# FFN weight scales from sums of squares of a second copy, and a reordered Strassen down phase with two-row-tile additions

## The chip, the core and the metric

The kernel is one program on one NeuronCore of a Trainium2 chip. The metric is the device time of one execution in microseconds (us), lower is better. The core has TensorE (PE, matrix products; its weight loads are shown as PEld), VectorE (DVE), ScalarE (ACT), GpSimd (POOL), and SyncE (SP), which here only issues DMAs. Every engine works through its own instructions in order and waits for the others by semaphores. The units' matmuls write PSUM, eight banks of 128 x 512 float32 numbers; DVE and ACT empty them.

## What is computed

One transformer block over 2048 tokens of width 576: pre-layernorm softmax attention with 32 heads of 18, and then a gated feed-forward network (FFN) of inner width 4608, each with a residual.

```python
h = x + _A_ref(_layernorm(x, axis=-1), A_wqkv, A_wo)
h2 = h + _B_ref(_layernorm(h, axis=-1), B_w_gate, B_w_up, B_w_down)

def _B_ref(x, w_gate, w_up, w_down):
    g = jnp.einsum("bsd,df->bsf", x, w_gate)
    u = jnp.einsum("bsd,df->bsf", x, w_up)
    h = _gelu(g) * u
    return jnp.einsum("bsf,fd->bsd", h, w_down)
```

The change lies in the FFN, and in the preparation of its scales beside the start of the attention.

## The kernel before

**Numbers.** Each float32 operand is multiplied by a power of two and cut into a float16 high part and a float16 rest, so that a product takes three float16 matmuls. The power of two of a weight block is found from its largest magnitude by `exponents`: DVE reduces (L129), a PE transpose of the column of maxima (L138), a second DVE reduce (L142), and some ten tiny integer operations.

**The loop.** The inner width is cut into 18 chunks of 256 columns; two chunks make one pass of the loop `for sc in range(9)`. The tokens are in two halves, p = 0 and p = 1. A full pass runs these stages in this order: `unit(c, 1)`, `unit(c + 1, 1)`, `down7(1)`, `unit(c + 2, 0)`, `unit(c + 3, 0)`, `down7(0)`, where c = 2 sc and the last three stages belong to the next pair of chunks. The first pass has the plain `down(1)` in place of `down7(1)`; the last one ends at `down7(1)`.

**A unit** multiplies half of the tokens by one chunk of the gate and the up matrix with seven Strassen products each: 14 products of 7 matmuls, alternating between gate (g) and up (u). They are numbered 0 to 13 below. Products 0, 4, 8 and 10 share PSUM bank g[0], products 1, 5, 9 and 11 share u[0]. Between them ACT copies the bank out: after product 0 to `xg` (L1198), after 1 to `xu` (L1201), after 4 to `ag` (L1213), after 5 to `au` (L1217), after 8 to `bg` (L1226), after 9 to `bu` (L1230). So product 10 waits until ACT has done the copy `bg`, and product 11 for the copy `bu`. ACT also applies gelu (L1180) and rounds seven results to their high parts (`high`, L1191); DVE adds, multiplies gate by up (L1183) and subtracts (last of all L1266 and L1267); POOL forms the seven rests (`low`, L1194). Six of the seven rests come behind product 11.

**A weight matrix** is loaded into the one buffer `W8` by `load_matrix` (eight DMAs on SP, L977 and L979; blocks A12, A22, A11, A21 in this order). POOL adds the four Strassen sums S1 to S4 (L993); the last one, S4, still reads A12. ACT rounds in three cuts (L1013: first the four loaded blocks' A12, A22, A11, then S1 and S2, then S3 and S4), DVE makes the rests (L1027, L1029). After the first cut's rests the load of the next matrix is issued into the same buffer. The rows of `w_down` use the same space (`load_down`, L1076); `split_down7` scales them (ACT L1136), forms sums (POOL L1138 to L1145), and cuts seven blocks (ACT L1132, DVE L1133).

**down7** multiplies by seven blocks of `w_down` for two row tiles at a time, 12 matmuls of 288 columns for a block, into three pairs of PSUM banks: X, B and Z. After each product DVE adds the bank to the running sum `nat` (L1291, or L1296 for two halves at once). Tiles of `nat` leave for DRAM (L1301), and the other half's come back (L1320).

**What sets the order.** PE, ACT, DVE, POOL and, in the FFN, SP run in the order in which the program text emits. `beside(main, side)` emits one step of the side work after each product of the unit. So the place where a side step is emitted is its place in the queue of every engine it uses. In the kernel before, the sums of the next gate matrix are formed beside `unit(c, 1)`, its cuts beside `unit(c + 1, 1)`, the rest of the splits is spread over `down7(1)` and the units of half 0, and `split_down7` stands in `unit(c + 3, 0)`.

## Time and profile before

| | us |
|---|---|
| median of 3 runs | 2756.2 |
| lowest and highest run | 2752.95, 2759.34 |
| the profiled execution's own time | 2758.85 |
| its span on the core | 2757.0 |

The profile is a record of one execution. A row of its timeline gives the start in us, the duration, the engine, the source line, the operation with its output and inputs, the number of instructions merged into the row, and in brackets the idle time before it and what ended that. A row of its table by stretches of time gives, for each stretch, its length, the busy time of PE, PEld, DVE, ACT and POOL with the number of instructions, the mean granted clock of PE, the share of the DMA engines, and GB/s. A row of its groups gives busy time and mean ns of one, and behind the bar the idle time of the engine before these instructions.

### The profile page before, as it was taken

Reading aid. Unit: us, or ns where it says so; the run is one execution under the profiler, and the core shown is the slowest. Engines: PE = TensorE matmul, PEld = TensorE weight load, DVE = VectorE, ACT = ScalarE, POOL = GpSimd, SP = SyncE. Lnnn points to the kernel's source line nnn. Section 1 sums busy time; section 2 is a strip of 40 time slices with the busy share of each in tenths; the row PEclk is TensorE's granted clock in tenths of the full one; section 3 lists DMA queues with packets and bytes.
Section 4 is the critical chain, followed back from the end, with each engine's and each line's share of the span. In section 5 each row is a group of like instructions: output and inputs, shape, how many; then the busy total and the mean of one; then the engine's idle time right before and its main releaser. Section 6 shows DMA issues by size and latency. Waiting matters only on the chain.

```text
span 2757.0 us, 54241 instructions
## 1 busy us (share of the span) xinstructions
PE 2594.8 (94%) x20381; PEld 1174.7 (43%) x20381; DVE 2321.2 (84%) x4230; ACT 1740.0 (63%) x3260; POOL 1034.9 (38%) x1274
## 2 busy tenths in 40 slices
PE   8999999999999999999999988898989898988989
PEld 4533333333333333333355545454445454544545
DVE  7479999999999999998676778788787878787885
ACT  6229999999999999997744334343343433343432
POOL 4202532323232323235853344444443334434432
PEclk9999999999999999999999999999999999999999
DMA  8521010101010101011344223222222223232212
GB/s 221 139 90 30 19 44 16 44 16 42 16 45 16 44 17 42 18 30 36 70 99 88 73 80 101 97 70 76 91 90 90 99 88 107 80 111 86 79 62 82
DMA packets 204761, 189.06 MB, mean 69 GB/s; under 512 B 92504, under 2 KB 151404, under 8 KB 204498
## 3 DMA queue, kind: packets, MB, share of 16 engines
q1 hardware_dynamic: 195758, 169.27, 20.6%
q0 software_dynamic: 8608, 16.33, 2.4%
q8 instruction: 159, 2.61, 0.4%
q14 instruction: 104, 0.85, 0.1%
q10 hardware_dynamic: 132, 0.01, 0.0%
HBM read 115.44 MB, written 50.40 MB: 60 GB/s over the span
## 4 chain that ended last, share of the span: by engine, by line
PE 70%; DVE 16%; issue 5%; ACT 3%; DMA 2%; POOL 2%; SPq 1%; DVEq 0%; ACTq 0%; POOLq 0%
PE bank L673 18%; PE more L1175 8%; PE bank L1175 7%; PE quad L615 7%; PE bank L615 6%; PE more L1286 4%; PE bank L1286 4%; PE quad L300 4%; PE quad L665 4%; PE bank L300 4%; PE bank L665 3%; DVE mx L625 3%; PE more L300 1%; DMA A<-in_B_w_up_dram 1%; DVE W L1029 1%
## 5 line engine op out<-in xcount | busy, mean ns | idle before, releaser
L667 ACT ACTIVATE WK<-quad 128x512 f32<-128x512 f32 x1170 | 656.3, 621 | 26.0 <-PE quad L665 23.6
L673 PE MATMUL bank<-WK,V 128*32 128x256 f32 x8192 | 607.7, 389 | 2.6 <-DVE nat L688 0.6
L625 DVE TENSOR_REDUCE mx<-quad 128x1 f32<-128x512 f32 x836 | 554.0, 685 | 9.0 <-PE quad L665 1.5
L667 ACT ACTIVATE WK<-bank 128x512 f32<-128x512 f32 x878 | 504.9, 622 | 12.0 <-PE bank L665 10.2
L625 DVE TENSOR_REDUCE mx<-bank 128x1 f32<-128x512 f32 x716 | 477.3, 685 | 35.5 <-PE bank L615 26.8
L1175 PEld LDWEIGHTS <-W 128*128 128x128 f16 x2394 | 242.6, 101 | 341.4 <-issue 85.5
L673 PEld LDWEIGHTS bank<-WK,V 128*32 128x32 f32 x8192 | 190.4, 109 | 268.5 <-issue 201.9
L698 POOL TENSOR_TENSOR rp<-rc,minus_one 128x4 f32<-128x4 f32 x112 | 111.2, 1012 | 380.1 <-DMA rc<-nat 377.9
L1175 PE MATMUL bank<-X,W 128*128 128x512 f16 x792 | 225.3, 382 | 0.0
L993 POOL TENSOR_TENSOR A<-A 128x384 f32<-128x384 f32 x136 | 142.7, 1065 | 193.3 <-DVE V L1208 99.3
L1175 PE MATMUL bank<-V,W 128*128 128x512 f16 x720 | 212.3, 395 | 0.5 <-ACT WK L1217 0.5
L615 PE MATMUL quad<-W 54*128 54x512 f16 x514 | 191.3, 383 | 0.0
L1286 PEld LDWEIGHTS <-WK 128*128 128x128 f16 x1472 | 147.3, 100 | 97.1 <-issue 54.2
L1286 PE MATMUL more<-nat,WK 128*128 128x288 f16 x736 | 142.4, 294 | 48.6 <-DVE nat L1291 48.6
L615 PEld LDWEIGHTS <-W 54*128 54x128 f16 x1024 | 74.5, 94 | 241.8 <-issue 227.5
L1013 ACT ACTIVATE W<-A,p_s_m 128x768 f16<-128x768 f32 (+1 forms) x78 | 79.0, 1036 | 149.1 <-DVE p_s_m L173 149.1
L665 PE MATMUL quad<-A 56*128 56x512 f16 x584 | 172.4, 381 | 0.3
L615 PE MATMUL quad<-A 54*128 54x512 f16 x462 | 171.8, 383 | 0.1
L615 PEld LDWEIGHTS <-A 54*128 54x128 f16 x1024 | 71.2, 94 | 231.5 <-issue 216.5
L665 PE MATMUL quad<-W 56*128 56x512 f16 x586 | 168.2, 382 | 0.1
L1175 PE MATMUL more<-V,W 128*128 128x512 f16 x414 | 125.3, 439 | 36.0 <-ACT nat L1226 16.9
L615 PE MATMUL bank<-A 54*128 54x512 f16 x442 | 152.3, 383 | 1.9 <-DMA A<-qk_hi 1.8
(460 smaller groups left out, 5136.7 us busy)
## 6 DMA issues: line engine op xcount, KB each, us to landing
nat_d<-nat SPq DMA_DIRECT2D x120, 288.0 KB
nat<-nat_d SPq DMA_DIRECT2D x120, 288.0 KB
A<-in_B_w_down_dram SPq DMA_DIRECT2D x8, 1152.0 KB
nat<-rc SPq DMA_DIRECT2D x32, 256.0 KB
A<-in_B_w_gate_dram SPq DMA_DIRECT2D x64, 128.0 KB
A<-in_B_w_up_dram SPq DMA_DIRECT2D x64, 128.0 KB
qk_hi<-tmp SPq DMA_DIRECT2D x36, 128.0 KB
qk_lo<-tmp SPq DMA_DIRECT2D x36, 128.0 KB
```

The source lines that it names most:

```text
L300: nc.tensor.matmul(dst, a, b, start=(i == 0), stop=(i == len(pairs) - 1))
L615: nc.tensor.matmul(pm[:, :TB], Q[r, q0 : q0 + P], keys, start=True, stop=True)
L625: nc.vector.tensor_reduce(dst, pm[:, :TB], axis=AX.X, op=ALU.max)
L665: nc.tensor.matmul(pS[:, :TB], K[r, kt * P : (kt + 1) * P], Q[r, qc * TB : (qc + 1) * TB], start=True, stop=True)
L667: nc.scalar.activation(pes[(2 * kt + hh // 2) % NPE][:, hh % 2], pS[:, :TB], AF.Exp, scale=ex_reg)
L673: nc.tensor.matmul(acc[32 * hh : 32 * hh + 32, qs], Vg[n // NB][:, kt * G4 + hh * VC : kt * G4 + hh * VC + 32], pes[(2 * kt + hh // 2) % N ...
L698: nc.gpsimd.tensor_tensor(rc[:, c : c + 4], den[:, c : c + 4], minus_one.to_broadcast([P, 4]), op=ALU.pow)
L993: op(W8[:, d], W8[:, a], W8[:, b])
L1013: by = hi_on or (lambda dst, src, k: nc.scalar.activation(dst, src, AF.Copy, scale=k))
L1029: nc.vector.scalar_tensor_tensor(wh[r, a:b, 2], W8[r, a:b, 2], s[r], wh[r, a:b, 2], op0=ALU.mult, op1=ALU.subtract)
L1175: nc.tensor.matmul(bank, w, x_, start=start and i == 0, stop=i == len(mm) - 1, skip_group_check=not start)
L1286: nc.tensor.matmul(bank[:, :HALF], a, b, start=start and k == 0, stop=k == len(mm) - 1, skip_group_check=not start)
```

## The change

Five things are changed.

1. The power of two of a gate, up or down block in chunks 2 and above comes from the sum of its squares instead of its largest magnitude. A second copy of the weights is loaded for it, squared in place by ACT with a sum along the row, and summed over the partitions by one matmul with ones. `scan_weights` does it for two gate and two up chunks beside `unit(c, 1)`, `scan_down` for the two down chunks beside `unit(c + 2, 0)`, both in the space of the `nat` tiles that are in DRAM at the time; those tiles are loaded behind it. `next_norms` does it for the chunks 2 and 3 beside the first attention maxima.
2. The splits of chunks 2 and above (`split_known`) contain no search for the exponent. Both splits of chunk c + 2, with the sums S1 to S4 of its gate matrix, are emitted beside `unit(c + 1, 1)`, both of chunk c + 3 beside `unit(c + 2, 0)`, and `split_down7` beside `unit(c + 3, 0)`.
3. No side work stands beside `down7` or `down`.
4. `down7` runs its products in another order, two of them cut in halves by the chunk they belong to. The two banks of a pair are neighbours in PSUM, and one addition takes both (two row tiles), except for HA12.
5. The loads of raw weights beside the attention maxima start earlier, and the side work there is taken in larger steps towards the end.

```diff
-    singles = [ps.tile([P, 512], F32, name=f"bank{i}") for i in range(4)]
+    bank4 = ps.tile([P, 4, 512], F32, name="bank")
+    singles = [bank4[:, i] for i in range(4)]
...
+    def frobenius(q, name):
+        n = q.shape[1]
+        pb = next(m_ring)
+        nc.tensor.matmul(pb[:, :n], ones, q, start=True, stop=True)
+        yield
...
+    def chunk_rows(dst, w, c, eng):
+        for h in range(2):
+            eng.dma_start(dst[64 * h : 64 * h + 64].rearrange("p (j f) -> p j f", f=P),
+                          w[:, c * FC + h * P : c * FC + (h + 1) * P].rearrange("(p j) f -> p j f", j=9))
...
+    def square(v, q):
+        nc.scalar.activation(v, v, AF.Square, accum_out=q)
...
+    def scan_weights(sc):
+        v = [view(nat1, 8 * D * i, (2 * D,)) for i in range(4)]
+        jobs = [(w, c) for w in (w_gate, w_up) for c in (2 * sc, 2 * sc + 1)]
+        q = small.tile([P, 4], F32, tag="fq4", name="fq_a")
+        for _ in range(2):
+            yield
+        for i in range(4):
+            chunk_rows(v[i], *jobs[i], nc.sync)
+            if i % 2:
+                yield
+        for _ in range(4):
+            yield
+        for i in range(4):
+            square(v[i], q[:, i : i + 1])
+            yield
+        for t in range(2 * TPB):
+            nc.sync.dma_start(nat[:, t], nat_d[:, 2 * TPB + t])
+        yield from frobenius(q, ("w", sc))
+
+    def scan_down(sc):
...
+        for _ in range(2):
+            yield
+        for i in range(2):
+            down_rows(v[i], 2 * sc + i, nc.sync)
+        for _ in range(5):
+            yield
+        for i in range(2):
+            square(v[i], q[:, i : i + 1])
+            yield
+        for t in range(2 * TPB):
+            nc.sync.dma_start(nat[:, t], nat_d[:, t])
+        yield from frobenius(q, ("d", sc))
...
+    def split_known(c, m, then, at=0, sums=True):
...
+        if sums:
+            form_sums()
+        high(0)
+        yield
+        for k, (a, b) in enumerate(cuts):
+            high(k + 1)
+            nc.vector.scalar_tensor_tensor(wl[:, a:b], W8[:, a:b, :2], s, wh[:, a:b, :2],
+                                           op0=ALU.mult, op1=ALU.subtract)
+            nc.vector.scalar_tensor_tensor(wh[r, a:b, 2], W8[r, a:b, 2], s[r], wh[r, a:b, 2],
+                                           op0=ALU.mult, op1=ALU.subtract)
+            if k == at:
+                then()
+            yield
...
     def split_down7(sc):
         df = view(A, W8O, (4, D))
-        ed = yield from exponents([view(A, W8O + 4 * 2 * D * i, (1, 2 * D)) for i in range(2)], "dn")
-        s = down_scale(ed, 266, -258)
+        e = exps[("w", sc)]
+        s = down_scale(exps[("d", sc)], (e[:, 0:2], e[:, 2:4]), 266, -268)
...
+        both = (0, 1)
         for i0 in range(0, TPB, 2):
-            for m, bs, start, n in ((HA11, Xs, True, 0), (HA22, Bs, True, 0), (HS1, Zs, True, 1),
-                                    (HS2, Xs, False, 1), (HA12, Bs, True, 0), (HS3, Xs, False, None),
-                                    (HS4, Zs, False, 1)):
+            j0 = TPB + i0
+            for m, bs, start, chunks in ((HA11, Xs, True, both), (HS1, Zs, True, (0,)), (HA12, Bs, True, (0,)),
+                                         (HS1, Zs, False, (1,)), (HS2, Xs, False, both),
+                                         (HA12, Bs, False, (1,)), (HS3, Xs, False, both),
+                                         (HS4, Zs, False, both), (HA22, Xs, False, both)):
                 for k in range(2):
...
+                    product(bs[k], m, i0 + k, start, chunks)
+                    if m == HA12 and 1 in chunks:
+                        add(bs[k][:, :HALF], j0 + k, 0)
+                    if k and 1 in chunks and m != HA12:
+                        t0, n = {HA11: (j0, 0), HS1: (i0, 1), HS2: (j0, 1), HS3: (i0, 1), HS4: (j0, 1),
+                                 HA22: (i0, 0)}[m]
+                        add((pair_x if bs is Xs else pair_z)[:, :, :HALF], slice(t0, t0 + 2), n)
                     yield
...
+        if sc == 0:
+            run(unit(c, 1))
+        elif not last:
+            beside(unit(c, 1), scan_weights(sc + 1))
...
+        side = chain((form_sums() for _ in range(1)), pause(1),
+                     split_known(c + 2, 0, lambda: load_matrix(w_up, c + 2), sums=False), pause(1),
+                     split_known(c + 2, 1, lambda: load_matrix(w_gate, c + 3)))
+        beside(u, side)
         run(side)
         if sc:
-            for i, _ in enumerate(down7(1, dsc, last, not last)):
-                if i >= 2 and i % 2 == 0:
-                    take(side)
+            run(down7(1, dsc, False))
...
+        side = chain(split_known(c + 3, 0, lambda: load_matrix(w_up, c + 3)), pause(1),
+                     split_known(c + 3, 1, lambda: load_down(sc + 1), 2))
+        ahead = scan_down(sc + 1) if sc else iter(())
+        for _ in unit(c + 2, 0):
+            take(side)
+            take(ahead)
+        run(side)
+        run(ahead)
+        dn = split_down7(sc + 1)
+        beside(unit(c + 3, 0), dn)
         run(dn)
```

More of the change, by code (lines that the diff above doesn't have):

```diff
@@ new lines, in next_norms, with fetch @@
+    def next_norms():
+        v = [w.rearrange("p a b -> p (a b)") for w in spare]
+        q = small.tile([P, 4], F32, tag="fq4", name="fq_a")
+        qd = small.tile([P, 2], F32, tag="fq2", name="fq_b")
+        jobs = [(1, w_gate, 2, q[:, 0:1]), (2, w_gate, 3, q[:, 1:2]), (3, w_up, 2, q[:, 2:3]),
+                (4, w_up, 3, q[:, 3:4]), (0, None, 2, qd[:, 0:1]), (1, None, 3, qd[:, 1:2])]
+        def fetch(i):
+            k, w, c, _ = jobs[i]
+            if w is None:
+                down_rows(v[k], c, nc.gpsimd)
+            else:
+                chunk_rows(v[k], w, c, nc.gpsimd)
+        for i in range(5):
+            fetch(i)
+        for _ in range(6):
+            yield
+        for i, (k, _, _, d) in enumerate(jobs):
+            square(v[k], d)
+            if i == 0:
+                fetch(5)
+            yield
+        yield from frobenius(q, ("w", 1))
+        yield
+        yield from frobenius(qd, ("d", 1))
@@ L1272, in unit, with down7, product @@
         yield
-    def down7(p, dsc, last, more):
+    def down7(p, dsc, last):
         Xs, Bs, Zs = ([banks[k], banks[3 + k]] for k in (1, 0, 2))
-        def product(bank, m, i, start):
+        def product(bank, m, i, start, chunks=(0, 1)):
             tsl = slice(i * P, (i + 1) * P)
             mm = []
-            for c in range(2):
+            for c in chunks:
                 w = slice(c * HALF, (c + 1) * HALF)
@@ L1495, in tile_block, with fetch_rows @@
-        beside(unit(c, 1), side, head=0 if sc else 7)
+        def fetch_rows(t0):
+            for t in range(2 * TPB):
+                nc.sync.dma_start(nat[:, t], nat_d[:, t0 + t])
+        if sc == 0:
+            run(unit(c, 1))
+        elif not last:
+            beside(unit(c, 1), scan_weights(sc + 1))
+        else:
+            beside(unit(c, 1), (fetch_rows(2 * TPB) for _ in range(1)))
+        u = unit(c + 1, 1)
+        if last:
+            run(u)
+            run(down7(1, dsc, True))
+            break
```

120 lines of the change are left out of this document (57 added, 63 removed).

## The prediction

> **What bounds the kernel now.** First the page, for which engine the time follows; then the table by stretches, one full pass of the loop cut where PE's rows change between L1175 (units) and L1286 (down7), with two stretches of the last pass, which has no side work.
>
> ```profile
> span 2757.0 us, 54241 instructions
> ...
> PE 70%; DVE 16%; issue 5%; ACT 3%; DMA 2%; POOL 2%; SPq 1%; DVEq 0%; ACTq 0%; POOLq 0%
> ```
>
> ```profile
> core 0: us, PE busy (x) PEld busy (x) DVE busy (x) ACT busy (x) POOL busy (x), PEclk, DMA share, GB/s
> 1627.43:1672.24 44.81, 43.01 (x200) 19.33 (x198) 28.59 (x50) 19.43 (x31) 16.46 (x13) 1.00 0.28 93
> 1672.24:1700.55 28.31, 22.66 (x171) 17.10 (x170) 26.88 (x49) 9.32 (x12) 11.77 (x10) 0.94 0.20 68
> 1700.55:1755.96 55.41, 46.79 (x201) 20.43 (x198) 45.87 (x73) 25.95 (x40) 24.13 (x18) 0.91 0.33 110
> 1755.96:1778.92 22.96, 20.74 (x170) 16.42 (x169) 20.13 (x33) 3.60 (x6) 10.82 (x9) 1.00 0.17 63
> ...
> 2687.53:2708.68 21.15, 21.15 (x100) 9.58 (x98) 7.48 (x11) 7.25 (x12) 2.31 (x2) 1.00 0.46 161
> ...
> 2730.53:2753.40 22.87, 20.90 (x169) 16.32 (x167) 19.66 (x33) 3.06 (x6) 6.96 (x5) 1.00 0.18 68
> ```
>
> A unit that nothing disturbs takes 21.15 us, 1.51 for each product (fifth row). A down7 has 168 matmuls; the rows below put 12 of them at 1.47, so 20.5. A pass then needs 4 x 21.15 + 2 x 20.5 = 125.6 and takes 151.5. PE loses 2.5 in the units of half 1, 7.8 in down7(1), 13.1 in the units of half 0, 2.5 in down7(0). DVE, at 26.88 of 28.31, is the bound of down7(1), where the splits stand; in down7(0) DVE is not full. The largest loss has rows of its own:
>
> ```profile
> 1733.04 0.69 PE L138 MATMUL more<-id,am_dn 128*128 128x128 f32 x2 [5.18 <-DVE am_dn L133]
> 1733.52 3.19 PE L1175 MATMUL more<-V,W 128*128 128x512 f16 x7
> 1736.50 2.37 PE L1175 MATMUL bank<-V,W 128*128 128x512 f16 x7
> ...
> 1737.80 2.40 ACT L1136 ACTIVATE A<-A,p_s_dn 128x1152 f32<-128x1152 f32 x2
> ...
> 1748.36 3.15 PE L1175 MATMUL more<-V,W 128*128 128x512 f16 x7 [3.44 <-ACT tmp L1226]
> ```
>
> The search for w_down's exponent holds PE for 5.18; the last row is product 10 held by a late copy bg, because ACT was in the split of w_down. **So a split costs PE time when it stands on ACT's queue ahead of the copies, not by its busy time.** That is what I follow through the new order, stage by stage. T is the start of a unit's first product.
>
> **Removed.** Eight reduces of 768, two of 1152 and their small operations go from DVE in each pass (eight of the first row below are 7.6 us), and the two waits of PE on a maximum.
>
> ```profile
> L129 DVE TENSOR_REDUCE ac_m<-A 128x1 f32<-128x768 f32 x56 | 52.4, 946 | 11.2 <-DMA A<-in_B_w_up_dram 10.9
> ...
> L155 ACT ACTIVATE A<-nat 128x576 f16<-128x576 f32 x5 | 3.4, 681 | 0.0
> ...
> L155 ACT ACTIVATION_READ_ACCUMULATOR A<-nat 128x1 f32 x5 | 1.0, 199 | 0.0
> ...
> L1013 ACT ACTIVATE W<-A,p_s_m 128x1152 f16<-128x1152 f32 x21 | 26.4, 1255 | 134.3 <-DVE p_s_m L173 134.3
> ...
> WK<-in_B_w_up_dram POOLq DMA_DIRECT2D x4, 288.0 KB, 11.5
> ```
>
> **Added: unit(c, 1) with scan_weights.** A square of 1152 is not in the trace: 1.26 by the same width in L1013 plus 0.20 for reading the sum, 1.45 (lower bound 0.88, the row of 576; upper 1.56, twice that row with one read). ACT does four behind products 8 to 11, and the matmul of `frobenius` stands behind product 12.
>
> ```profile
> 2701.38 0.58 ACT L1226 COPY tmp<-more 128x512 f32<-128x512 f32 x1 [3.95 <-PE more L1175]
> ...
> 2703.32 0.72 ACT L1180 ACTIVATE tmp<-tmp,p_gsc 128x512 f32<-128x512 f32 x1
> ...
> 2714.79 0.58 ACT L1198 COPY V<-more 128x512 f32<-128x512 f32 x1
> ...
> 2715.21 1.16 POOL L1194 TENSOR_TENSOR WK<-V,WK 128x512 f16<-128x512 f32 x1
> ...
> 2715.42 1.24 PE L1175 MATMUL more<-V,W 128*128 128x512 f16 x5 [0.53 <-ACT V L1198]
> ```
>
> Copy bg begins at T + 13.85 (first row). From there ACT has two copies, two gelus and a rounding (I put it at a copy's 0.58), 3.2, and 5.8 of squares, to T + 22.8; PE has ended product 12 at T + 19.6 and waits 3.2. I take **+2.5**, as ACT's rows overlap a little when they follow each other, between 0 (squares hidden) and +5: the eight loads go out on SP as the last tiles leave, and with the 11.5 of the nearest load row they land about as ACT asks. The reload of nat behind them has until down7(1), over 20 us, and is hidden; on SP it stands ahead of the next load, which comes 20 us later.
>
> **unit(c + 1, 1) with two splits.** The sums S1 to S4 stood beside unit(c, 1); now they queue on POOL behind that unit's last rest, which ends at 2716.37, 7.7 after this unit's first product (2708.68, the end of the undisturbed stretch above).
>
> ```profile
> 1655.28 1.26 ACT L1013 ACTIVATE A<-A,p_s_m 128x1152 f16<-128x1152 f32 x1
> ...
> 1657.65 0.38 SPq L977 DMA_DIRECT2D A<-in_B_w_up_dram  x1
> ...
> 1660.66 0.45 SPq L977 DMA_DIRECT2D A<-in_B_w_up_dram  x1
> ...
> 1661.93 0.45 SPq L977 DMA_DIRECT2D A<-in_B_w_up_dram  x1
> ...
> 1666.40 4.44 POOL L993 TENSOR_TENSOR A<-A 128x384 f32<-128x384 f32 x4 [2.56 <-DMA A<-in_B_w_up_dram]
> ```
>
> Sums take 4.44, so S4 lets the first DMA of the up matrix go at T + 12.1. A load takes 8.75 from its first issue to the sums that waited for it (1657.65 to 1666.40): landed at T + 20.9, the three blocks of the first cut 1.27 earlier (1660.66 to 1661.93, the issues of the last two blocks). That cut stands on ACT behind product 7, ahead of copy bg. ACT is held until T + 19.6, cuts to 20.9, has copied bg at 21.5: product 10, due at T + 15.6, waits 5.9. The second cut, 768 wide and some 0.9, needs S2, two more sums (T + 23.1), and stands before copy bu, done at T + 24.6: product 11, due at 23.0, waits 1.6. With 0.5 at product 4, as now (last row of the fence before), the unit loses 8.0. The pair takes 42.3 + 2.5 + 8.0 = 52.8, **+8.0** against 44.81. Were ACT free in time, it would be +0.5: the low end.
>
> **The down phases.** The additions fall from twelve of 288 and two of 576 to two of 288 and six of 576:
>
> ```profile
> 2730.53 0.53 PE L1286 MATMUL more<-nat,WK 128*128 128x288 f16 x3
> ...
> 2732.00 0.53 PE L1286 MATMUL more<-nat,WK 128*128 128x288 f16 x3
> ...
> 2734.54 1.64 DVE L1267 TENSOR_TENSOR A<-nat,tmp 128x512 f32<-128x512 f32 x1
> ...
> 2736.10 0.51 DVE L1291 SCALAR_TENSOR_TENSOR nat<-more,p_dsc,nat 128x288 f32<-128x288 f32 x1
> ...
> 2736.66 0.53 PE L1286 MATMUL more<-nat,WK 128*128 128x288 f16 x3 [1.56 <-DVE nat L1291]
> ...
> 2740.53 0.82 DVE L1296 SCALAR_TENSOR_TENSOR nat<-more,p_dsc,nat 128x576 f32<-128x576 f32 x1
> ```
>
> That saves DVE 12 x 0.51 + 2 x 0.82 - 2 x 0.51 - 6 x 0.82 = 1.8 for two tiles, 3.6 a call. But PE waits for the first addition, behind the unit's last subtraction, 5.6 after the start. Now X is wanted again after 36 matmuls (4.4) and one addition of 0.51. The new order wants it after 30 (3.67), and its addition takes 0.82: ready at 6.5, 2.8 late. Then X comes back after 6 matmuls (0.73) where latency and addition take 1.05, twice 0.3 late, and at once from HA22 to the next HA11, 1.05 late. Sum 20.5 + 2.8 + 0.6 + 1.05 = 25.0 in the undisturbed case, against 22.87. **down7(0): +2.0** against 22.96 (0 to +3). In down7(1) the tail comes later, since two rests of the up matrix also fall behind the held copies: by 2.9 at most, two of the 1.45 of a rest below, by 0 at least; I take 2.1, so 27.1: **-1.2** against 28.31 (-3.3 to -0.4).
>
> **unit(c + 2, 0) with two splits and scan_down.** The sums are done in down7(1). The first cut follows product 0 and copy xg (T + 2.2), and the load goes out 2.4 later (1655.28 to 1657.65), at 4.6; it lands at 13.3, the sums end at 17.7. On ACT, in program order: first cut to 13.3, second (S2 at 15.5) to 16.4, third (S4) to 18.6, square to 20.1, copy bg to 20.7. Product 10 is due at 15.1. The matmul of frobenius stands before it and waits for the second square, 22.1, so product 10 starts at 22.3: the unit takes 28.3 (low end 21.2).
>
> **unit(c + 3, 0) with split_down7.** It runs from 1721.65 to 1755.96 now, and ACT L1136 starts 16 into it. Without the search it waits for the DVE tail (5.6) and ten small operations (1.7, the first two rows below): T + 7.5. But copy au (after product 5) stands behind high(A22), which waits for the gate on DVE, behind 2.4 of scaling (L1136), a rounding of 0.6, four rests of 1.45 and three operations of the unit of 0.8: T + 18.7; two roundings and the copy, 0.6 each, end at 20.5. Product 9, due at 13.6, waits; five products more make 28.1 (21.2 to 34).
>
> ```profile
> 1735.79 0.15 DVE L1100 CUSTOM_DVE_ANT_0 E<-ee 128x4 uint16<-128x4 uint16 x1
> ...
> 1737.29 0.17 DVE L173 TENSOR_SCALAR p_s_dn<-pi_s_dn 128x2 int32<-128x2 int32 x1
> ...
> L1133 DVE TENSOR_TENSOR nat<-A,nat 128x576 f16<-128x576 f32 x49 | 68.2, 1446 | 26.4 <-ACT nat L1132 26.4
> ```
>
> The pair is 56.4, **+1.0** against 55.41.
>
> **The start.** Six squares (8.7) and their loads come into the first maxima, where ACT is a third busy and PE full:
>
> ```profile
> 120.00:140.00 20.00, 20.00 (x146) 12.07 (x143) 15.36 (x30) 7.31 (x24) 0.00 (x0) 1.00 0.49 103
> ...
> L1180 ACT ACT_TABLE_LOAD x1 | 1.3, 1283 | 0.0
> ```
>
> Work hidden; but the side steps go by twice as fast, and a DVE reduce can meet a load that has not landed (11.5): **+4** (0 to 10).
>
> **Sum.** A pass: 8.0 - 1.2 + 1.0 + 2.0 = +9.8; seven full passes +69. The first pass has no scans but the same holds: +4. Of the last only down7 changes: +2. With the start +79: 2758.85 + 79 = 2838 for an execution like the profiled one, which lies 2.65 above the median; so **2835**.
>
> A half-rate PE is left out of the sum: after the idle 5.18 above, seven matmuls took 2.98 and the next 2.2, together 2.2 too long. The Trainium skill's page "TensorE: Matmul & The Clock Gate", Part 1, says that an idle window of about 3.4 us halves the clock until PE has been busy as long; the row agrees. Two holds longer than that in a pass would by the row give up to 7 x 4.4 = 31 more; I leave it out as ACT is behind anyway, and in the upper end.
>
> **The rivals.** (a) One hold only: up lands in time in one of the two units, or the w_down unit comes clean (21.2): a pass of about +3, 2785; 0.16. (b) Faster: no hold at all. Pass: 45.3 + 25.0 + 21.2 + 28.1 + 25.0 = 144.6, -6.9; seven are -48, with +10 elsewhere 2718. It is decided by whether the up matrix lands before copy bg is due (T + 13.6): I work out 20.9 in one unit and 13.2, then sums, in the other. For it speaks the DVE time freed; 0.15. (c) Squares cost a table load on ACT (1283 ns, row above) and another back to gelu: some eight a pass, 9 us, 2898; 0.04. The page "ScalarE: Activation LUTs", Table sets, names relu, copy, identity and abs as in every set, not Square; no FFN row shows a Square. (d) The holds only change places and the gains pay for them, within 0.2% (about what a measurement of this kernel can tell from no change): 0.03. The forecast, 2795 to 2890, has 0.62.
>
> Slower 0.62 + 0.16 + 0.04 = 0.82, same 0.03, faster 0.15. The range 2740 to 2890 leaves out most of (b) and (c), some 0.17; its top is the sum with the half-rate and the late scan loads.
>
> **What would show it.** Product 10 held by copy bg in the two split units, 5 to 7 us each; ACT's first cut of the up matrix waiting on its DMA; no PE wait on a maximum; down7(0) near 25 with four short holds on the additions; frobenius holding PE under 3. I am wrong if the split units stay near 21.5, which means that ACT was not waiting for the load.

## The result and the profile after

The changed kernel takes 5610.8 us (median of 4 runs, 5605.0 to 5616.3) against 2755.4 for the kernel before in runs beside it: 2.036 times as long, with a 95% interval of 2.0325 to 2.0395. The forecast was 2835, within 2740 to 2890. The side was right, the size was not: what doubles the time is not in the sum at all.

The head of the page of the changed kernel, first, and its costliest group:

```profile
span 5611.1 us, 54460 instructions
...
PEclk9765555555555555555555555566999998999899
...
L674 PE MATMUL bank<-WK,V 128*32 128x256 f32 x8192 | 1031.9, 624 | 359.1 <-DVE mx L626 199.7
```

The same group in the kernel before:

```profile
L673 PE MATMUL bank<-WK,V 128*32 128x256 f32 x8192 | 607.7, 389 | 2.6 <-DVE nat L688 0.6
```

The clock row tells where to look: in 23 of the 40 slices PE is granted half its clock, in four more 0.6 to 0.7, and these slices are the attention, which the change hardly touches. L674 (L673 before) multiplies the softmax weights by the values there. The first matmul of the first unit ends the attention. Here it is in the kernel before, and then in the changed one:

```profile
1399.62 1.67 PE L1175 MATMUL more<-X,A 128*128 128x512 f16 x7 [0.61 <-DVE nat L799]
```

```profile
3950.27 1.67 PE L1292 MATMUL more<-X,A 128*128 128x512 f16 x7 [0.61 <-DVE nat L800]
```

So 2550.7 of the 2854.1 us come before the FFN, and the FFN itself goes from 1357.4 (2757.0 - 1399.6) to 1660.8. The table by stretches of the changed kernel has one stretch of the attention, and one full pass of the loop in the order down7(1), units of half 0, down7(0), units of half 1 (the line of a unit's matmuls is now L1292, that of down7 L1403):

```profile
2000.00:3000.00 1000.00, 685.37 (x3408) 140.32 (x3407) 347.19 (x587) 352.15 (x641) 93.42 (x160) 0.51 0.03 9
...
4297.55:4324.15 26.60, 21.54 (x169) 16.41 (x168) 14.29 (x19) 2.05 (x4) 9.62 (x9) 1.00 0.12 45
4324.15:4394.43 70.28, 50.23 (x201) 20.89 (x199) 44.15 (x67) 32.25 (x50) 23.39 (x19) 0.88 0.31 105
4394.43:4421.02 26.59, 21.53 (x169) 16.40 (x168) 14.28 (x19) 2.04 (x4) 5.77 (x5) 1.00 0.12 45
4421.02:4481.43 60.41, 45.98 (x200) 19.68 (x198) 32.46 (x49) 28.21 (x45) 19.86 (x18) 0.94 0.45 122
```

In the attention nothing is full: PE is busy 685 of 1000 us at a clock of 0.51, DVE and ACT about 350 each. An attention in which every engine idles is one that waits. The timeline of the changed kernel shows on what (L616 makes scores for the maxima, L626 reduces them on DVE, L666 makes the scores again, L668 takes exp on ACT):

```profile
1002.18 0.60 PE L616 MATMUL bank<-W 54*128 54x512 f16 x1
1002.89 0.69 DVE L626 TENSOR_REDUCE mx<-bank 128x1 f32<-128x512 f32 x1 [1.78 <-PE bank L616]
1003.63 0.58 PE L666 MATMUL bank<-W 56*128 56x512 f16 x1 [0.85 <-DVE mx L626]
...
1004.25 0.60 ACT L668 ACTIVATE WK<-bank 128x512 f32<-128x512 f32 x1 [3.11 <-PE bank L666]
1004.90 0.58 PE L666 MATMUL bank<-W 56*128 56x512 f16 x1 [0.69 <-ACT WK L668]
```

Matmul, reader, matmul, reader, matmul: some 1.3 us for each step, although each of these three matmuls writes another bank. The waits of the two kernels, in us in total, number and longest, first of the kernel before in its attention, then of the changed one:

```profile
PE bank L665 <- ACT WK L667: 0.6, 1, 0.6
PE bank L665 <- DVE mx L625: 0.4, 1, 0.4
```

```profile
PE bank L666 <- DVE mx L626: 229.2, 278, 1.2
...
PE bank L674 <- DVE mx L626: 199.7, 274, 0.8
...
PE bank L666 <- ACT WK L668: 172.9, 225, 2.3
```

Two waits have become 503. The matmuls L616 and L666 take their banks in turn from a ring of seven, three of them in the tile, so that one has to wait only for the reader of its own bank, seven uses of the ring back; in the rows above it waits for the reader of the matmul just before. The wait of L674 is plainer still: it writes the fourth bank of the tile, which L626 does not read in this loop, and waits for L626 274 times. All that the attention's banks saw of the change are its first lines, which make the four banks `singles` views of one tile.

### The profile page after: what moved, and what is told of

Its sections match the earlier page's. It is cut to its first block, busy times and chain, and to the rows that moved or that the text cites. A ratio compares the mean times of both kernels' runs of the same rounds, so it can differ in the third digit from the quotient of the medians.

```text
span 5611.1 us, 54460 instructions
## 1 busy us (share of the span) xinstructions
PE 4001.5 (71%) x20365; PEld 1323.6 (24%) x20365; DVE 2308.5 (41%) x3839; ACT 1912.7 (34%) x3356; POOL 1003.6 (18%) x1284
## 5 line engine op out<-in xcount | busy, mean ns | idle before, releaser
L674 PE MATMUL bank<-WK,V 128*32 128x256 f32 x8192 | 1031.9, 624 | 359.1 <-DVE mx L626 199.7
L668 ACT ACTIVATE WK<-quad 128x512 f32<-128x512 f32 x1170 | 646.3, 597 | 1118.0 <-PE quad L666 1053.7
L626 DVE TENSOR_REDUCE mx<-quad 128x1 f32<-128x512 f32 x836 | 573.7, 690 | 1033.8 <-PE quad L666 539.7
L626 DVE TENSOR_REDUCE mx<-bank 128x1 f32<-128x512 f32 x716 | 494.8, 691 | 1022.2 <-PE bank L616 730.2
L668 ACT ACTIVATE WK<-bank 128x512 f32<-128x512 f32 x878 | 525.2, 598 | 1142.7 <-PE bank L666 662.3
L674 PEld LDWEIGHTS bank<-WK,V 128*32 128x32 f32 x8192 | 255.0, 148 | 1255.1 <-DVE mx L626 569.4
L666 PE MATMUL bank<-A 56*128 56x512 f16 x440 | 259.0, 589 | 239.0 <-DVE mx L626 122.1
L666 PE MATMUL bank<-W 56*128 56x512 f16 x438 | 253.9, 580 | 226.7 <-DVE mx L626 107.1
L1292 PEld LDWEIGHTS <-W 128*128 128x128 f16 x2394 | 245.5, 103 | 550.2 <-issue 312.2
L616 PE MATMUL bank<-A 54*128 54x512 f16 x442 | 244.8, 554 | 162.7 <-ACT WK L668 75.3
L616 PE MATMUL bank<-W 54*128 54x512 f16 x382 | 223.7, 586 | 120.1 <-ACT WK L668 85.9
L616 PE MATMUL quad<-W 54*128 54x512 f16 x514 | 305.1, 607 | 0.0
L666 PE MATMUL quad<-A 56*128 56x512 f16 x584 | 292.2, 612 | 0.0
L666 PE MATMUL quad<-W 56*128 56x512 f16 x586 | 285.6, 605 | 0.0
L616 PE MATMUL quad<-A 54*128 54x512 f16 x462 | 275.0, 610 | 0.0
L1292 PE MATMUL bank<-X,W 128*128 128x512 f16 x558 | 170.3, 428 | 106.6 <-ACT tmp L1318 32.5
L616 PEld LDWEIGHTS <-W 54*128 54x128 f16 x1024 | 96.0, 112 | 631.5 <-issue 630.9
L616 PEld LDWEIGHTS <-A 54*128 54x128 f16 x1024 | 93.8, 110 | 637.8 <-issue 634.1
L1403 PE MATMUL bank<-nat,WK 128*128 128x288 f16 x992 | 178.9, 286 | 63.7 <-DVE nat L1409 63.7
L1292 PE MATMUL more<-X,W 128*128 128x512 f16 x702 | 192.5, 379 | 36.0 <-DVE V L1367 7.0
```

The source lines that it names most:

```text
L616: nc.tensor.matmul(pm[:, :TB], Q[r, q0 : q0 + P], keys, start=True, stop=True)
L626: nc.vector.tensor_reduce(dst, pm[:, :TB], axis=AX.X, op=ALU.max)
L666: nc.tensor.matmul(pS[:, :TB], K[r, kt * P : (kt + 1) * P], Q[r, qc * TB : (qc + 1) * TB], start=True, stop=True)
L668: nc.scalar.activation(pes[(2 * kt + hh // 2) % NPE][:, hh % 2], pS[:, :TB], AF.Exp, scale=ex_reg)
L674: nc.tensor.matmul(acc[32 * hh : 32 * hh + 32, qs], Vg[n // NB][:, kt * G4 + hh * VC : kt * G4 + hh * VC + 32], pes[(2 * kt + hh // 2) % N ...
L1292: nc.tensor.matmul(bank, w, x_, start=start and i == 0, stop=i == len(mm) - 1, skip_group_check=not start)
```

## The experiments

### One tile for four banks, in the kernel before

```diff
-    singles = [ps.tile([P, 512], F32, name=f"bank{i}") for i in range(4)]
+    bank4 = ps.tile([P, 4, 512], F32, name="bank")
+    singles = [bank4[:, i] for i in range(4)]
...
-    more = [ps2.tile([P, 512], F32, name=f"more{i}") for i in range(4)]
+    more4 = ps2.tile([P, 4, 512], F32, name="more")
+    more = [more4[:, i] for i in range(4)]
```

> The kernel before, with the four PSUM banks "bank" made one tile of four banks and the four banks "more" of the FFN another, and nothing else changed. Theory: a matmul into one bank of such a tile waits for the readers of its other banks, and a reader waits for matmuls into the other banks, and this alone doubles the time: 5000 to 5700 us, the attention (200 to 1380 us before) about 3.0 times as long, PE waiting for the DVE reduces (L625) and ACT exponentials (L667) of other banks. Rival: the tiles cost nothing and the lost time comes from the scans, splits or the new order in the FFN and from the loads and squares beside the maxima: within 1% of 2755 us.

Measured: 5506.3 us, in a single run, against 2758.2. Its attention, in the table by stretches:

```profile
200.00:3923.00 3723.00, 2561.84 (x12752) 563.01 (x12751) 1301.37 (x2238) 1277.18 (x2323) 422.44 (x688) 0.54 0.05 12
```

The first unit starts at 3943.79 here. Nothing but the allocation differs, so the tile alone makes the doubling.

### The changed kernel with a tile for each bank

The eight banks are tiles of their own again; an addition over two tiles at once is then not possible, so each pair addition becomes two single ones, each right behind its product.

```diff
-                    if k and 1 in chunks and m != HA12:
+                    if 1 in chunks and m != HA12:
...
-                        add((pair_x if bs is Xs else pair_z)[:, :, :HALF], slice(t0, t0 + 2), n)
+                        add(bs[k][:, :HALF], t0 + k, n)
```

> The changed kernel, with eight PSUM tiles of one bank each as before, and so with the pair additions of down7 made as two additions of one row tile, each right behind its product. Theory: the doubling goes away and what is left is the rest of the change. By the prediction's steps (ACT held by the load of the up matrix in the two split units, frobenius, the later start of down7's second X product) 2800 to 2890 us, with unit(c+1,1) and unit(c+2,0) each 5 to 8 us longer than 21.2 and down7(0) 24 to 25. Rival 1: ACT is not held and the freed DVE time counts: 2680 to 2745 us. Rival 2: the doubling is not the tiles' doing: above 5000 us.

Measured: 2870.6 us, a ratio of 1.0396 (1.0375 to 1.0417). That is the change without its tile, and what the forecast was about. Its table by stretches, one full pass from the units of half 1 on:

```profile
1809.00:1862.89 53.89, 45.74 (x200) 19.92 (x198) 31.84 (x46) 26.26 (x42) 20.66 (x17) 0.90 0.48 127
1862.89:1890.86 27.97, 23.86 (x170) 17.59 (x169) 20.99 (x35) 3.60 (x6) 10.81 (x9) 0.88 0.17 62
1890.86:1953.11 62.25, 47.81 (x201) 20.61 (x199) 41.78 (x67) 31.41 (x48) 23.51 (x18) 0.92 0.34 115
1953.11:1976.08 22.97, 20.77 (x170) 16.42 (x169) 18.30 (x31) 3.02 (x6) 6.96 (x5) 1.00 0.17 63
```

And its timeline, rows of four engines (L1070 loads a matrix, L1137 is a split's cut on ACT, L1342 the copy bg, L972 the matmul of frobenius, L992 the square, L1317 the copy xu):

```profile
1830.27 0.39 PE L972 MATMUL bank<-fq_a,ones 128*128 128x4 f32 x2 [1.46 <-ACT nat L992]
...
1844.28 0.38 SPq L1070 DMA_DIRECT2D A<-in_B_w_up_dram  x1
...
1852.20 1.25 ACT L1137 ACTIVATE W<-A,p_s_m 128x1152 f16<-128x1152 f32 x1 [7.40 <-DMA A<-in_B_w_up_dram]
1853.37 0.57 ACT L1342 COPY V<-more 128x512 f32<-128x512 f32 x1
...
1853.98 3.14 PE L1291 MATMUL more<-V,W 128*128 128x512 f16 x7 [6.69 <-ACT V L1342]
1857.02 3.01 PE L1291 MATMUL bank<-V,W 128*128 128x512 f16 x7
...
1912.11 0.59 PE L972 MATMUL more<-fq_b,ones 128*128 128x2 f32 x2 [5.98 <-ACT nat L992]
1912.56 3.15 PE L1291 MATMUL more<-V,A 128*128 128x512 f16 x7
...
1933.38 1.67 PE L1291 MATMUL bank<-V,W 128*128 128x512 f16 x7 [3.80 <-ACT tmp L1317]
```

The reader is to see the hold of the forecast: ACT stands 7.40 us before a cut whose matrix has not landed, the copy bg stands behind that cut, and product 10 waits 6.69 for the copy. Frobenius for w_down holds PE for 5.98 ahead of product 10 of `unit(c + 2, 0)`. Behind the first hold the rows of products 10 and 11 read 3.14 and 3.01, where that of an undisturbed one reads 1.67.

### The new order of the down phase, alone in the kernel before

The product table and the additions of the diff, with single additions, and nothing else.

> The kernel before, with only down7's products in the new order, additions of one row tile each. By the prediction's count X is wanted again 30 matmuls after its first product instead of 36, so each of the eight down7(0) waits some 0.7 us longer for the first addition and about 1 us at the end of a pair of row tiles: about 1.5 us longer, and down7(1), with the splits beside it, 0 to 2 us longer: 2765 to 2785 us. Rival: the halves of HS1 and HA12 that need only the older unit cover the tail of the newer one, and the new order is 1 to 3 us a call faster: 2710 to 2740 us.

Measured: 2827.2 us, 1.0255 (1.0237 to 1.0272). A miss for both: the order costs 69 us (2827.2 - 2758.2) where the theory had some 10 to 30. Its down7(1), against 28.31 before, and its down7(0), in the table by stretches:

```profile
1831.07:1867.74 36.67, 26.39 (x170) 18.59 (x169) 31.75 (x61) 9.32 (x12) 15.48 (x14) 0.86 0.26 87
...
1924.39:1947.36 22.97, 20.78 (x170) 16.42 (x169) 18.30 (x31) 3.02 (x6) 10.82 (x9) 1.00 0.16 63
```

Down7(0), where no split stands, takes 22.97 against 22.96. In down7(1) the side steps are taken in every second of now 36 steps instead of 28, and DVE's busy time there goes from 26.88 to 31.75.

### Own tiles in the attention only

```diff
-    bank4 = ps.tile([P, 4, 512], F32, name="bank")
-    singles = [bank4[:, i] for i in range(4)]
+    singles = [psp.tile([P, 512], F32, name=f"bank{i}") for i in range(4)]
...
+    bank4 = ps2.tile([P, 4, 512], F32, name="bank")
+    singles = [bank4[:, i] for i in range(4)]
     more4 = ps2.tile([P, 4, 512], F32, name="more")
```

> The changed kernel with four one-bank tiles in the attention and the two tiles of four banks only from the FFN on. Theory (banks of one tile wait for each other's readers wherever the tile is): the attention comes back to its 1180 us, the FFN keeps its 1831 us: 5611 - 2400 = 3210, between 3150 and 3270, with half-0 units near 70 and half-1 units near 60. Rival (the loss of the attention comes from the new first-maxima work or from the clock and not from the tile): above 5000. Rival (the tile costs nothing in the FFN, and its 1831 us come from the splits alone): 2860 to 2890, as with own tiles everywhere.

Measured: 3068.8 us, in a single run, below the expected 3150. The expectation had cut the changed kernel's FFN at 3780 us, 170 too early. By the first unit's start its FFN takes 1660.8, and in this run (first unit at 1405.89):

```profile
200.00:1380.00 1180.00, 1169.79 (x12350) 388.88 (x12347) 1119.41 (x2118) 1133.10 (x2278) 418.93 (x679) 1.00 0.13 33
1405.89:3066.00 1660.11, 1265.68 (x6740) 673.27 (x6740) 911.08 (x1391) 568.24 (x884) 521.59 (x481) 0.94 0.28 86
```

The attention is whole again at clock 1.00; the FFN is that of the changed kernel. So of the tile's cost 2542 us (5610.8 - 3068.8) lie in the attention, and 198 (3068.8 - 2870.6) in the FFN, there together with the pair additions, which the run with own tiles does not have.

### The second split three products later

Own tiles, and both splits of the up matrix later, that of w_down as well.

```diff
-                     split_known(c + 2, 0, lambda: load_matrix(w_up, c + 2), sums=False), pause(1),
+                     split_known(c + 2, 0, lambda: load_matrix(w_up, c + 2), sums=False), pause(4),
...
-        side = chain(split_known(c + 3, 0, lambda: load_matrix(w_up, c + 3)), pause(1),
+        side = chain(split_known(c + 3, 0, lambda: load_matrix(w_up, c + 3)), pause(4),
...
-        dn = split_down7(sc + 1)
+        dn = chain(pause(3), split_down7(sc + 1))
```

> Own tiles everywhere (as in the run of 2870.6), and the split of the up matrix put three products later in both split units, the split of w_down three products later as well. Theory (ACT's cut waits for the load of the up matrix ahead of copies bg and bu, which holds product 10): the hold of 6.7 us and the two products at half rate behind it (2.9) go from the half-1 pair, and most of 6.0 + 2.4 from the half-0 pair; what is late next is the end of the unit, some 3 us: a pass 10 to 15 shorter, seven 70 to 105: 2765 to 2800. Rival (PE waits for the load itself or for DVE's rests, not for ACT's queue): the hold moves to the next stage whole and the time stays within 2850 to 2880.

Measured: 2848.8 us, 1.0329 (1.0312 to 1.0346), far above the theory's 2765 to 2800 and just under the rival's 2850. The table by stretches (units of half 1, down7(1)) and the timeline:

```profile
1803.55:1847.72 44.17, 42.71 (x200) 19.31 (x198) 26.47 (x41) 24.47 (x40) 14.23 (x12) 1.00 0.56 145
1847.72:1879.41 31.69, 23.23 (x169) 17.37 (x168) 26.23 (x39) 5.70 (x9) 18.49 (x14) 0.89 0.20 68
```

```profile
1848.19 5.85 POOL L1124 TENSOR_TENSOR A<-A 128x384 f32<-128x384 f32 x4 [8.48 <-DMA A<-in_B_w_up_dram]
1854.00 1.33 POOL L1310 TENSOR_TENSOR W<-V,W 128x512 f16<-128x512 f32 x1
...
1855.39 0.42 PE L1402 MATMUL bank<-nat,W 128*128 128x288 f16 x1 [6.89 <-POOL W L1310]
...
1894.37 1.16 ACT L992 ACTIVATE nat<-nat 128x1152 f32<-128x1152 f32 x1 [5.05 <-DMA nat<-in_B_w_down_dram]
```

The hold by ACT's queue is shown, for the units lose 53.89 - 44.17 = 9.7 us: hold and slow products together. But much of it comes back at once in down7(1), 27.97 to 31.69 here and up to 34.5 in other passes: now POOL waits 8.48 with the sums of the late matrix, the units' rests stand behind them, and down7 needs the rests. The load comes no earlier, so the wait goes to the next queue that has its work ahead of the unit's. In half 0 a square waits for its rows in the same way, 5.05.

### Without the scans

The loop's squares, their loads and frobenius are taken out; the second pass's scales serve all later ones.

> Own tiles everywhere (as in the run of 2870.6), without the squares, their loads and the matmul of frobenius in the loop: the scales of the second pass are used for all later ones (the scales of the later chunks are left out). Theory (the scans are a minor term; the wait on the late copy bg stays): the half-1 pair loses the hold of 1.5 on frobenius, the half-0 pair 2 to 3 of its 6.0: a pass 3.5 to 4.5 shorter, seven 25 to 32: 2838 to 2846. Rival (the scans are the main cost of the FFN): under 2800. Rival (covered by the other holds): 2860 to 2875.

Measured: 2840.2 us, 1.0306 (1.0289 to 1.0323), as expected: the scans are some 30 (2870.6 - 2840.2) of the 112 us that the change costs with own tiles (2870.6 - 2758.2).

### Tiles of two banks

A tile for each bank in the attention; in the FFN only the two banks of each pair share a tile, and the pair additions are kept.

```diff
+    pair_x = ps2.tile([P, 2, 512], F32, name="bank")
+    singles = [pair_x[:, i] for i in range(2)] + [ps2.tile([P, 512], F32, name=f"bank{i}") for i in (2, 3)]
+    pair_z = ps2.tile([P, 2, 512], F32, name="more")
+    more = [pair_z[:, i] for i in range(2)] + [ps2.tile([P, 512], F32, name=f"more{i}") for i in (2, 3)]
```

> The changed kernel with one-bank tiles in the attention, and in the FFN only the two banks of a pair addition in one tile (two tiles of two banks, four of one). Theory (a reader of one bank holds the next matmul into the other): product 3 of every unit waits for the addition to xg on DVE, some 0.5 to 1.0 in each of some 32 units, and the down phases wait for additions of 0.82 instead of 0.51: 2880 to 2920. Rival (the additions over two row tiles save DVE 3.6 a call and pay for that): 2840 to 2868.

Measured: 2938.7 us, 1.0664 (1.0635 to 1.0692), 68 above own tiles and more than expected. Its waits, a row of its timeline, and its stretches of down7(1) and down7(0):

```profile
PE bank L1291 <- DVE tmp L1320: 39.6, 10, 10.8
PE bank L1291 <- DVE nat L1320: 32.5, 3, 10.8
```

```profile
1965.22 3.15 PE L1291 MATMUL bank<-X,W 128*128 128x512 f16 x7 [10.83 <-DVE tmp L1320]
```

```profile
1895.36:1918.50 23.14, 21.89 (x170) 16.79 (x169) 13.24 (x19) 1.82 (x3) 8.77 (x9) 0.96 0.14 52
...
1984.48:2007.70 23.22, 21.22 (x169) 16.41 (x168) 14.00 (x19) 2.05 (x4) 5.78 (x5) 1.00 0.14 52
```

L1320 reads g[1], product 3 writes u[1], its neighbour in the tile. Product 3 needs nothing from that reader and waits for it, 0.85 to 1.3 us where DVE is prompt and 10.83 where it stands in the split of w_down. The down phases gain: down7(1) falls from 27.97 to 23.14. The units, 53.89 to 58.27 and 62.25 to 65.98 in the same table, lose more. Some 25 of the 68 us lie ahead of the full passes: from the first unit to the first down phase of half 0 the run takes 238.0 us, against 212.8 with own tiles.

### Half 0: squares later, the split of w_down spread out

As the run of 2848.8, with `scan_down`'s squares behind products 12 and 13, its frobenius behind the unit, and a step of `split_down7` in every second product from product 4 on.

> As the run of 2848.8 (own tiles, second split three products later), with the two squares of scan_down behind products 12 and 13 (8 and 9 before), frobenius behind the unit, and the split of w_down from product 4 on in every second step. Theory (in the half-0 pair too PE waits because ACT's queue holds something that waits, the square for its rows of w_down and the rounding for POOL, ahead of the copies): the holds of 4.9 and of 8.9 and the half-rate products behind them go, the pair falls from 62 to between 45 and 50, a pass by 12 to 17: 2725 to 2770. Rival (the hold only moves on, into down7(0), as it moved from half 1 to down7(1) in the run before): 2825 to 2850.

Measured: 2836.2 us, 1.0284 (1.0264 to 1.0304), within the rival's range: the half-0 pair falls from 62.6 to 55.6, and down7(0) rises from 24.7 to 29.3. Part of the wait went on to DVE: the unit's last additions, which empty banks that down7(0) writes, now stand behind rests of w_down, and PE waits 2.23 and 3.18 for them. In the pair, frobenius now comes behind product 0 of the next unit and holds PE there for 10.12.

### Scans one pass ahead

The squares of the weights are taken a pass earlier, so that the sums of the gate can stand ahead of `unit(c, 1)` and its split at the head of `unit(c + 1, 1)`. Against the run before, in part:

```diff
+        if not last:
+            form_sums()
...
-            beside(unit(c, 1), scan_weights(sc + 1))
+            beside(unit(c, 1), scan_weights(sc + 2))
...
-        side = chain((form_sums() for _ in range(1)), pause(1),
-                     split_known(c + 2, 0, lambda: load_matrix(w_up, c + 2), sums=False), pause(4),
+        side = chain(split_known(c + 2, 0, lambda: load_matrix(w_up, c + 2), sums=False), pause(5),
```

> As the run before it in this list, with the squares of the weights taken one pass earlier (those of the second pass at the start too), so that the sums of the gate stand ahead of unit(c, 1) and its split begins with unit(c + 1, 1). Theory (the load of the up matrix comes too late, as the sums and the first cut before it come late; whatever in-order queue has its work ahead of the unit's is held: ACT in the changed kernel, POOL's rests in the run of 2848.8): the load goes out at T + 5 instead of T + 12, nothing waits for it, down7(1) falls from 34 to 25 to 28, seven or eight passes by 6 to 9 each, with 3 to 8 more at the start: 40 to 65 below the run before it, near 2700. Rival (the load's time is set by the DMAs themselves or by DVE's rests of the cut): within 15 of the run before it.

Measured: 2818.1 us, 1.0215 (1.0192 to 1.0238), 18 below the run before it: less than the theory's 40 to 65, more than the rival's 15. Down7(1), and a row of the timeline:

```profile
1837.29:1865.33 28.04, 22.68 (x169) 16.93 (x168) 23.41 (x40) 4.83 (x8) 12.85 (x11) 0.94 0.23 77
```

```profile
1898.60 0.59 PE L972 MATMUL more<-fq_b,ones 128*128 128x2 f32 x2 [10.44 <-ACT nat L992]
```

With the load earlier, down7(1) does come down, to 28.0 in the pass shown, from 31.2 in the run before. But frobenius for w_down, behind product 0 of the next unit as in that run, meets a square that ACT has not reached, and holds PE for 10.44.

### The new order with its side steps spread

The kernel before with the new order, as above, and 13 side steps over the 36 steps of down7(1), as many as before over 28.

> The kernel before with the new order of the down phases and single additions, as in the run of 2827.2, but the side steps of down7(1) taken 13 times spread over the 36 steps, as many as before over 28. Theory (the splits were drawn forward by the steps and held the additions on DVE): down7(1) falls from 35.7 to between 28 and 30, seven passes by 6 to 8: 2770 to 2790. Rival (the new order itself meets the tail of the units worse when DVE is full): 2810 to 2830.

Measured: 2810.3 us, 1.0201 (1.0166 to 1.0236), at the foot of the rival's range: 53 us are left of the 69, so some 16 are the density of the steps (5 to 27 by the two intervals). Its down7(1) and down7(0), and the longest wait of PE for the additions in the first:

```profile
1833.40:1867.07 33.67, 24.23 (x170) 17.74 (x169) 28.45 (x50) 9.32 (x12) 12.21 (x10) 0.90 0.19 62
...
1922.68:1949.27 26.59, 23.66 (x169) 17.61 (x168) 19.52 (x33) 3.60 (x6) 10.83 (x9) 0.87 0.17 61
```

```profile
PE more L1286 <- DVE nat L1292: 6.9, 3, 3.8
```

Down7(1) still takes 5.4 us more than before, and down7(0) now 3.6 more. The kernel before waited 5.1 in down7(1) for these additions, in two, so this wait explains 1.8 of the 5.4. It fits the new order asking for its X banks sooner while the additions come late behind splits on DVE; how the rest divides is not settled.

### Two last orders

As the run of 2818.1, but the first puts the squares of w_down two products earlier, their frobenius behind product 2 of the next unit, the second split of half 0 one product earlier, and the split of w_down in one piece from product 8 on. The second is the same with the old order of the down phases.

> As the run of 2818.1 (squares of the weights one pass ahead), with the squares of scan_down two products earlier, its matmul of frobenius behind product 2 of the next unit (it held PE for 10.4 us behind product 0), the split of the up matrix one product earlier and the split of w_down in one piece from product 8 on, when its load has come. Theory (nothing on an in-order queue stands ahead of its data any more, only the chain gate split, load, up split, load, w_down split through one buffer is left): the half-0 pair falls from 56 to between 45 and 48, down7(0) rises from 29.5 to about 31, as DVE ends the split later: seven passes by 7 to 10: 2745 to 2770. Rival (the chain sets the sum of both stages, so that down7(0) takes back what the units win): 2795 to 2820.

> As the run before it in this list, with the down phases in the order of the kernel before. Theory (the new order wants X's additions sooner, so that it loses where DVE comes late, in both down phases here): each call 2 to 4 us shorter, 16 calls 30 to 60: 2700 to 2735. Rival (the order costs nothing beside splits that are placed well, as down7(1) at 27.9 and down7(0) at 22.97 with the changed kernel's splits had it): within 10 of the run before it.

Measured: 2825.2 us, 1.0242 (1.0222 to 1.0261), and 2829.0, 1.0255 (1.0237 to 1.0273). The first lies above both its ranges and 7 above the run it starts from: frobenius for w_down holds PE no more, but product 4 of `unit(c + 3, 0)` waits in its place, since the copy xg stands behind the roundings of the unit before:

```profile
1905.79 3.07 PE L1302 MATMUL more<-V,W 128*128 128x512 f16 x7 [5.01 <-ACT tmp L1325]
```

The second gives the same time within 4 us: with these splits the order matters little. No version came below 2755; the nearest ones are 2810 (the new order in the kernel before) and 2818 (scans a pass ahead).

## Why the prediction was right and wrong

**The step that failed is one that the sum does not contain.** The sum was made of "a pass", "the first pass", "the last" and "the start", and the only step that reached the attention was the start, with "Work hidden". The first lines of the diff were taken as a name for memory. They cost 2542 us in the attention and, with the pair additions, 198 in the FFN. The front of this document says that the two banks of a pair are neighbours "and one addition takes both"; that a tile is also the unit by which a matmul waits for a reader was not asked, neither for the attention, which shares `singles`, nor for the units. That the side was right owes nothing to this step: what the sum did see is 112 of the 2855 us.

**The FFN without the tile** can be laid beside the forecast, stage by stage, for the pass shown of each run:

| us | before | forecast | own tiles | two banks | as changed |
|---|---|---|---|---|---|
| units, half 1 | 44.8 | 52.8 | 53.9 | 58.3 | 60.4 |
| down7(1) | 28.3 | 27.1 | 28.0 | 23.1 | 26.6 |
| units, half 0 | 55.4 | 56.4 | 62.3 | 66.0 | 70.3 |
| down7(0) | 23.0 | 25.0 | 23.0 | 23.2 | 26.6 |
| a pass | 151.5 | 161.3 | 167.1 | 170.6 | 183.9 |

- **unit(c + 1, 1): right, in its mechanism and nearly in its times.** T is 1832.0 there. The load was to go out at T + 12.1 and went at T + 12.3 (1844.28); product 10 was to wait 5.9 and waited 6.69. Product 11, which was to wait 1.6, did not. What the sum lacks is the half rate behind the hold, which the prediction left to the upper end of its range: products 10 and 11 have rows of 3.14 and 3.01 instead of 1.67. The half rate followed the holds of 6.69 and 5.98, and not that of 3.80 (1.67 for seven matmuls); but behind the hold of 3.80 in another pass, at 2098.39, the seven took 2.88. The Trainium skill's page "TensorE: Matmul & The Clock Gate", Part 1, puts the halving at an idle window of about 3.4 us.
- **unit(c, 1) with its scan: right in kind.** Frobenius held PE 1.46, for a forecast of 2.5 between 0 and 5.
- **unit(c + 2, 0): right, but for the half rate.** Product 10 was to start at T + 22.3, and started at T + 21.7 (1912.56). Products 10 and 11 took 5.6 us (to 1918.15), 2.6 more than the sum had.
- **unit(c + 3, 0): wrong in place and size.** The copy au was to be late behind the split of w_down; already xu was, behind its scaling, and after it ag and au. The unit took 31.9 (1921.2 to 1953.1) instead of 28.1.
- **down7(0): wrong in this version, for no addition over two tiles is left in it.** With tiles of two banks it takes 23.2 instead of 25.0: the short holds come (0.9 us at most), but the long one of 2.8 behind the unit's last subtraction is 0.74, as the unit's last two subtractions take 0.68 each there instead of the 1.64 that the forecast had from the trace before.
- **down7(1): a gain of 1.2 forecast, 0.3 found** with own tiles, 5.2 with tiles of two.
- **The start: right.** The first unit starts at 1405.69 with own tiles instead of 1399.62, +6.1 for a forecast of +4.

The rivals: the one on table loads is out, as the changed kernel has three loads of tables on ACT, just as the kernel before. Those of no hold at all and of one hold only are out too, by the 6.69 and the 5.98, and with them that of no change.

Together the sum was +79, with the 4 of the start, and the change without its tile is +112 (2870.6 - 2758.2), of which the half-0 pair alone makes 7 x 5.9 = 41 more than forecast and down7(0) 14 less. The range would have held it; it could not hold the change as it stands.

## What to carry to other kernels

If an edit joins buffers into one tile so that one instruction can reach them all, go through every other user of that memory, in every stage, and ask which of its writes will now wait for a reader of another part. A wait on an in-order queue that stands ahead of its data is only in part removed by moving it later: in three of the runs here some of it went on, to POOL, to the work on DVE ahead of down7(0), to the next unit. The units of half 1 and their down7(1) together took 80.7 us in the mean of the seven full passes with own tiles, 77.2 with the later split, and 73.9 when the load itself came earlier. Compare first where a known mark of the program (here the first unit) starts in both traces; that would have shown in one line that the doubling lies in a stage that the sum left out.

## What the runs showed of the hardware

**Short waits are enough to keep PE at half its clock.** In the changed kernel's attention PE is never idle for longer than 1.22 us between 1000 and 3000 us, though idle in some 850 places, yet the granted clock there is 0.52 and 0.51, and the matmuls of L674 take 624 ns over the whole attention where the kernel before has 389. With own tiles in the attention the waits are gone, and the clock is 1.00. The Trainium skill's page "TensorE: Matmul & The Clock Gate" speaks of an idle window of about 3.4 us in its Part 1. Its section "A second HAM failure mode: psum-queue depth-cycling" says that small idle times between groups of matmuls make the clock go back and forth. The second is nearer to this trace, though the clock here stays near half. For single holds no length is settled: with own tiles every hold of 5.98 us and more was followed by the half rate, and behind the eight holds of 3.80 the next matmuls came between 216 and 419 ns apart. Which share of the attention's 2542 us is the clock and which the waits was not taken apart.

**DVE is slower beside POOL.** Groups of the run with own tiles, 512 wide: the first is the subtraction of the unit's tail with POOL forming rests beside it, the second, from PSUM, reads only one operand from SBUF, and the third is the subtraction again with POOL idle:

```profile
L1382 DVE TENSOR_TENSOR V<-nat,V 128x512 f32<-128x512 f32 x4 | 6.6, 1642 | 0.0
...
L1374 DVE TENSOR_TENSOR V<-more,V 128x512 f32<-128x512 f32 x9 | 6.2, 692 | 10.0 <-PE more L1291 10.0
...
L1382 DVE TENSOR_TENSOR A<-WK,A 128x512 f32<-128x512 f32 x4 | 2.7, 679 | 0.0
```

In that run 25 of the 32 executions of L1382 began while POOL was in an operation, and each took 1.63 to 1.64 us; the other 7 took 0.68. In the run with tiles of two banks none of the 32 began so, and all took 0.68 to 0.69. Eight of the nine of the second group began beside POOL and took 0.69 all the same. The Trainium skill's page "SBUF — State Buffer", section "SBUF: two separate sides", says that DVE and GpSimd share a pair of ports, which one of them holds for a whole instruction, where a DVE operation has two operands in SBUF. The 1642 against 679 agree, and so does the 692 of the one with an operand in PSUM. So the tail of a unit, two subtractions of this kind, is 1.9 us longer where both begin while POOL is at the rests.
